# A sigmoid-attention, Fourier-mixing and feed-forward kernel: weight blocks start later, stores are put back, a shorter reciprocal root, one load for queries and keys, and another order of the first chunk's weight sums

## The chip, the cores and the metric

The kernel runs on one core of one Trainium2 chip. A core has five instruction streams that run on their own and meet at semaphores: TensorE (PE; its weight loads are listed as PEld), VectorE (DVE), ScalarE (ACT), GpSimd (POOL) and SyncE (SP), which here only issues transfers. Sixteen DMA engines carry the transfers. Each stream works in program order. The metric is the time of one execution on the device, in microseconds; lower is better.

## What is computed

There are 8 batches of 448 tokens, 12 heads of 64, a model width of 768 and a hidden width of 3072, all in float32.

```python
scores = scale * np.matmul(q, k.transpose(0, 1, 3, 2)) - np.log(S)
attn = 1.0 / (1.0 + np.exp(-scores))          # a sigmoid, no softmax
x = np.matmul(attn, v)                        # heads put side by side: [8, 448, 768]
mixed = np.real(np.fft.fft(np.fft.fft(x, axis=1), axis=2))
u = x + mixed
un = (u - mean(u)) / np.sqrt(var(u) + 1e-06)
out = u + np.maximum(un @ w_ch1, 0.0) @ w_ch2
```

## The kernel before

The program is one function. It has three stages on PE: attention with the Fourier mixing, a first chunk of 512 token rows in plain matrix products, and six further chunks in a scheme with seven products in place of eight.

**Attention runs in passes.** A pass is one group of two head pairs (gg), numbered from 0; there are 24, three to a batch. A pass is eight steps of a counter t, two to a turn of the loop at line 541. In the turns PE computes the scores (half_scores, scores), ACT their sigmoid, and PE the values of the pass before (half_values, values). Other work is put into a table of steps, at(t, fn), and each turn emits what stands there for its two steps. pin() then ties every instruction to the one before it on the same engine, SP included, so the order of emission is the order of execution on each stream.

Four kinds of work stand in that table.

*Queries and keys.* load_qk(g) brings one half group, keys and queries in two transfers, on SP (on ACT for g = 1). There are four buffers of each. cast (ACT, and DVE or POOL for the first two) rounds them, rest (DVE, line 119) keeps the remainder; the products of rounded and remainder parts make the scores.

*Weight blocks.* There are 48, 24 of each matrix. weight(n, step) handles one. Step 0 is SP's load of 768 KB into a buffer wr (four of them). Step 1, on ACT (line 300), takes the absolute values into a buffer wt (four, shared with the tiles hl of the normalization). Step 2, on DVE (line 305), takes the maximum over the block. Step 3, on DVE (lines 309, 312, 314), is three integer operations that put a float32 together, called the shifts here. Step 4 (line 317) is SP's store of 384 KB to t_dram. A block is named by its end, the step t of its shifts; ends lists t with the distances of the five steps from it. Before, there are three families: one end each eighth step from 11 on, one each eighth from 16 on, and one each 24th from 30 on. They are ordered by t, and the first 48 are used. After the last come weight_top (the maximum over all, DVE and a POOL all-reduce) at TP and weight_scales four steps later. pair loads two blocks back and splits them into a high and a low float16 part.

*Folds and mixing.* POOL folds the outputs of a batch (fold, lines 194 to 200). mix_units(b) lists the matrix products of the two Fourier transforms in small units; mix_some emits some 4.9 us of them at step 4 of a pass. Their constants are cd, cs and ident, loaded at steps 18 and 22; cs has 113 rows. The results are tiles u (three buffers), which SP stores to u_dram. sp_next holds these stores until flush(sp_next), which comes at the start of each turn.

*Normalization of chunk 0.* Two half chunks, at steps 96 and 120 and the 20 after each: norm loads u (n = 0), takes statistics (n = 1), the reciprocal root rsqrt (n = 2 to 6), scales (n = 7), splits into hl (n = 8 on ACT, line 401; n = 9 on DVE, line 405) and transposes by DMA on SP (line 407). rsqrt starts from an integer trick and makes four Newton rounds of four DVE operations each on 128 x 2 elements. fast_norm does the same for the later chunks, twice a chunk.

**The first chunk.** For each of 24 hidden blocks f, up_proj makes 18 products, evac the relu (ACT) and its low part (DVE), down_proj 24 products four blocks later. prepare(k) runs twice per block, at k = 2f and 2f + 1, called half steps, and takes the steps of pair due then from plan: load, high part (ACT, line 435), low part (DVE, line 437), four sums in place on POOL (line 445), high and low part of the sums, store to w_dram. The distances from 4p are listed in line 636; the second matrix (i = 1) follows 5 later. The rest of the last batch's mixing runs between the first four blocks (mix_rest). PSUM has two banks for up_proj and for the transposes of fast_norm (ps_h).

**The further chunks.** fast_up and fast_down run 28 products to a group; DVE and ACT combine their results, and fast_norm prepares the next chunk.

Of the kernel before, what the change touches and what calls it, by code (L numbers as in the profile page):

```python
# [9 lines left out]
F32 = mybir.dt.float32  # L10
# [3 lines left out]
ALU = mybir.AluOpType  # L14
# [4 lines left out]
S = 448  # L19
# [3 lines left out]
D = 64  # L23
# [28 lines left out]

def spectral_attention_ffn(tc, q, k, v, w1, w2, cd, cs, ident_in, out):
    nc = tc.nc
    B = q.shape[0]
    NT = B * S
# [5 lines left out]
    with ExitStack() as top:  # L62
# [19 lines left out]
        if True:  # L82
# [11 lines left out]

            def load_qk(g):
                b, n = divmod(g, 2 * NG)
                qr = io.tile([128, SQ], F32, tag="qr", name="qr", bufs=4)
                kr = io.tile([128, S], F32, tag="kr", name="kr", bufs=4)
                e = nc.scalar if g == 1 else nc.sync
                e.dma_start(kr, k[b, n])  # L100
                e.dma_start(qr, q[b, n])
                raw[g] = (qr, kr)

# [99 lines left out]
            def mix_units(b):  # L203
# [32 lines left out]
                def add_x(kp, r, hf):  # L236

                    lo, hi = (1, HM - 1) if r and not kp else (0, HM - kp)
                    s, d = sd[kp]
                    if hf == 0:  # L240
                        if kp and r:
                            flush(sp_next)
                        ut[kp, r] = fx.tile([128, DM], F32, tag="u", name="u", bufs=3)
                    u = ut[kp, r]
                    ps = ps_m.tile([128, 512], F32, tag="m", name="psx")
                    for i in range(3):
                        nc.tensor.transpose(
                            ps[:HM - kp, i * 128:(i + 1) * 128], xT[:, hf * 3 + i, r, kp:HS:2], ident)
                    y = d if hf == r else s
                    m = HM - kp  # L250
                    ysl = y[:m, 384:0:-1] if hf else y[:m, 0:384]

                    def add():
                        nc.vector.tensor_tensor(
                            out=u[:m, hf * 384:hf * 384 + 384], in0=ps[:m, :384], in1=ysl, op=ALU.add)
                        if hf:
                            base = b * S + (0, 113, 225, 336)[2 * r + kp] - lo

                            cut = lo + (hi - lo) // 16 * 16
                            for i, j in ((lo, cut), (cut, hi)):  # L260
                                if i < j:
                                    sp_next.append(lambda i=i, j=j: nc.sync.dma_start(
                                        u_dram[base + i:base + j, :], u[i:j, :]))
                    dve_next.append(add)
# [91 lines left out]
            def rsqrt(c, n):  # L356
                mv = mvs[c]
                a, r, t = (mv[:, n] for n in range(2, 5))
                if n == 2:
# [8 lines left out]
                    return  # L368
                k = UN_SCALE if n == 6 else 1.0
                nc.vector.tensor_tensor(out=t, in0=r, in1=r, op=ALU.mult)  # L370
                nc.vector.tensor_tensor(out=t, in0=t, in1=a, op=ALU.mult)
                nc.vector.tensor_scalar(  # L372
                    out=t, in0=t, scalar1=-0.5 * k, scalar2=1.5 * k, op0=ALU.mult, op1=ALU.add)
                nc.vector.tensor_tensor(out=r, in0=r, in1=t, op=ALU.mult)

# [6 lines left out]
            def norm(c, i, n, pool):  # L382
# [6 lines left out]
                elif n == 1:  # L389
                    stats(c, i % 2, uns[c, i])  # L390
                elif n < 7:
                    rsqrt(c, n)
# [16 lines left out]
            def norm_plan(c, g, pool):  # L409

                res = [(0, lambda: norm(c, 2 * g, 0, pool))]
                for j in range(2):
                    for n, t in ((1, 6 + j), (7, 10 + j), (8, 16 + 2 * j), (9, 18 + 2 * j)):
                        res += [(t, lambda i=2 * g + j, n=n: norm(c, i, n, pool))]
                res += [(8 + n // 4, lambda n=n: norm(c, 2 * g, n, pool)) for n in range(2, 7)]
                return sorted(res, key=lambda x: x[0])
# [71 lines left out]

            load_qk(0)
            load_qk(1)  # L490
            load_v(0)
            for g in range(2):
# [3 lines left out]
                rest(g, 1)  # L496
            load_qk(2)
            load_qk(3)
            load_v(1)
            TQ = 4 * G  # L500
            TP = TQ - 16
            extra = {}
# [10 lines left out]
            for gg in range(1, GG):  # L513
                if gg > 1:
                    at(8 * gg - 4, lambda n=gg: load_v(n))
                    at(8 * gg - 14, lambda g=2 * gg: load_qk(g))
                    at(8 * gg - 13, lambda g=2 * gg + 1: load_qk(g))
                for w in range(2):
                    for n, fn in enumerate((cast, rest)):
                        at(8 * gg - 4 + 2 * n + 2 * w, lambda g=2 * gg + w, fn=fn: (fn(g, 0), fn(g, 1)))  # L520
            at(18, lambda: nc.sync.dma_start(cd_sb, cd))
            at(22, lambda: (nc.sync.dma_start(cs_sb, cs), nc.sync.dma_start(ident, ident_in)))
            ends = sorted([(t, (-8, -3, -1, 0, 2)) for t in range(11, TP + 2, 8)]
                          + [(t, (-8, -5, -2, 0, 2)) for t in range(16, TP + 2, 8)]
                          + [(t, (-8, -4, -2, 0, 2)) for t in range(30, TP + 2, 24)])
            for n, (t, ds) in enumerate(ends[:2 * NFC]):
# [4 lines left out]
            at(TP + 4, weight_scales)  # L531
            for p, d in ((0, 0), (1, 3)):
                for step, e in enumerate((0, 8 + 4 * p, 9 + 4 * p)):
                    at(TP + d + e, lambda p=p, step=step: pair(0, p, step))
# [6 lines left out]
            for t in range(0, TQ + 12, 2):  # L541
                flush(sp_next)
                gg, part = divmod(t // 2, 4)
# [21 lines left out]
        with ExitStack() as fast, ExitStack() as st:  # L565
# [61 lines left out]
            def mix_rest(us):  # L627
                flush(sp_next)
                flush(act_next)
                flush(dve_next)  # L630
                mix_some(us)

            plan = {}
            for p in range(NP):
                for i in range(2):
                    for step, d in enumerate((-7, -4, -3, -2, -1, 0, 2)):
                        if i == 0 and p < 2 and step < 3:
                            continue
                        plan.setdefault(max(4 * p + d + 5 * i, min(step, 2)), []).append((step, i, p))

# [36 lines left out]
            def fast_norm(c, tp, n, ps_pool):  # L677
# [11 lines left out]
                if n < 3:  # L689
                    stats(c, n - 1, rows[n - 1])  # L690
                elif n < 8:
                    rsqrt(c, n - 1)
                elif n < 10:
                    scale_rows(c, n - 8, rows[n - 8])
# [259 lines left out]
def _layout(q, k, v, w1, w2):  # L954
# [5 lines left out]
    n = np.arange(HS)  # L960
    qt, kt = (np.ascontiguousarray(a) for a in (qt[..., np.concatenate([n, -n % S])], kt))
    vt = v.reshape(B, 2, NG, 2, S, D)
# [18 lines left out]
    for kp in range(2):  # L981
        ang = (n[:, None] * np.arange(kp, HS, 2)) % S
        half = np.where(n % 112 == 0, 0.5, 1.0)[:, None]
        for c, fn in enumerate((np.cos, np.sin)):
            m = fn(2 * np.pi * ang / S) * half
            m[(ang + 112 * (1 - c)) % 224 == 0] = 0.0
            cs[:, kp, c, :HM - kp] = m
    return {"q_in": qt, "k_in": kt, "v_in": vt, "w1_in": w1t, "w2_in": w2t, "cd_in": cd, "cs_in": cs,
            "id_in": np.eye(128, dtype=np.float32)}
# [28 lines left out]
```

## Time and profile before

| | us |
|---|---|
| median of 3 runs | 1635.09 |
| lowest and highest | 1633.77, 1635.5 |
| the profiled execution | 1633.69 |
| its span, first to last instruction | 1631.9 |
| PE busy | 1579.4 (97%) |
| DVE busy | 1290.7 (79%) |
| ACT busy | 676.3 (41%) |
| POOL busy | 286.9 (18%) |

The times count one execution; the profile is another single execution, so sums made from its rows are compared with its own time. All times in rows are microseconds from the start of the span unless ns is written. The table of busy time by stretch gives for each stretch its length, then the busy time and, in brackets, the number of instructions of PE, PEld, DVE, ACT and POOL, then the granted PE clock as a share of full speed, the DMA engines' mean busy share and the GB/s moved. A line of the timeline gives start, duration, engine, line of the kernel, operation, output and input, count, and in square brackets how long the engine had been idle and what ended that. A group's line gives busy time, mean ns of one, and the idle time before it. The DMA lines give KB and the median time from issue to landing. SPq is the instruction with which SP issues a transfer.

### The profile page before, as it was taken

What the parts mean: (1) busy time and instruction counts of PE and PEld (TensorE: products, weight loads), DVE (VectorE), ACT (ScalarE), POOL (GpSimd) and SP (SyncE); (2) the same over time, 40 slices, a digit from 0 to 9 for tenths busy, and PEclk for the clock granted to TensorE, in tenths of its full rate; (3) what the DMA queues carried; (4) which work ended last, traced back from release to release, by engine and by line L of the source; (5) the groups of instructions that cost most, each with busy time, mean ns of one, the idle gap of its engine ahead of it and who ended that gap; (6) DMA issues with size and microseconds to landing.
All of it is one profiled execution on the core that took longest, in us unless ns stands there. A gap on an engine that the chain in (4) does not pass through costs nothing.

```text
span 1631.9 us, 28066 instructions
## 1 busy us (share of the span) xinstructions
PE 1579.4 (97%) x11176; PEld 1084.1 (66%) x11176; DVE 1290.7 (79%) x2527; ACT 676.3 (41%) x903; POOL 286.9 (18%) x245
## 2 busy tenths in 40 slices
PE   8699988899998999999999999999999999999998
PEld 3355655465654557777777777777777777777775
DVE  6687798874687865788878888888889888887778
ACT  7577766576345441423233323332333233323221
POOL 3334433344677640000000000000000000000000
PEclk9799999999999999999999999999999999999999
DMA  8788978872587886555566657564756475656561
GB/s 283 245 294 290 313 227 285 284 264 87 196 329 285 301 313 269 213 208 228 219 244 221 242 185 280 206 257 154 304 199 231 180 280 208 238 204 242 204 255 60
DMA packets 85557, 388.68 MB, mean 238 GB/s; under 512 B 14913, under 2 KB 28466, under 8 KB 66866
## 3 DMA queue, kind: packets, MB, share of 16 engines
q1 hardware_dynamic: 85138, 386.43, 64.8%
q8 instruction: 87, 1.43, 0.3%
q10 hardware_dynamic: 288, 0.46, 0.1%
q14 instruction: 44, 0.36, 0.1%
HBM read 311.36 MB, written 73.92 MB: 236 GB/s over the span
## 4 chain that ended last, share of the span: by engine, by line
PE 66%; DVE 4%; POOL 1%; issue 1%; ACT 1%; DMA 0%; ACTq 0%; DVEq 0%; POOLq 0%
PE pso L826 29%; PE psf L770 29%; PE po L600 4%; PE psh L580 3%; DVE wp L437 1%; POOL wq L445 1%; PE pst L699 1%; DVE F L776 1%; DVE H L776 0%; ACT H L805 0%; DVE ur L621 0%; DVE ur L854 0%; DVE mv L370 0%; DVE acc L903 0%; DVE mv L372 0%
## 5 line engine op out<-in xcount | busy, mean ns | idle before, releaser
L826 PE MATMUL pso<-ws,H 128*128 128x384 f16 x3024 | 507.5, 326 | 1.0 <-DVE H L776 0.9
L770 PE MATMUL psf<-ut,ws 128*128 128x256 f16 x4536 | 506.6, 273 | 1.2 <-DVE ur L621 1.2
L770 PEld LDWEIGHTS <-ws 128*128 128x128 f16 x4536 | 443.8, 98 | 60.3 <-issue 1.7
L826 PEld LDWEIGHTS <-H 128*128 128x128 f16 x3024 | 295.6, 98 | 186.9 <-DVE H L776 1.7
L795 ACT ACTIVATE F<-F 128x1024 f32<-128x1024 f32 x72 | 76.1, 1056 | 400.7 <-DVE F L776 400.7
L841 DVE TENSOR_TENSOR acc<-pso,acc 128x384 f32<-128x384 f32 x399 | 206.9, 548 | 21.7 <-PE pso L826 21.7
L776 DVE TENSOR_TENSOR H<-F,H 128x1024 f16<-128x1024 f32 (+1 forms) x144 | 155.2, 1086 | 54.3 <-ACT H L805 54.3
L124 ACT ACTIVATE a<-sc 128x900 f32<-128x900 f32 x168 | 147.3, 920 | 56.7 <-PE sc L136 50.1
L805 ACT ACTIVATE H<-F 128x1792 f16<-128x1792 f32 x72 | 122.2, 1697 | 106.7 <-DVE F L776 106.7
L776 DVE TENSOR_TENSOR F<-X,psf 128x256 f32<-128x256 f32 x288 | 117.3, 417 | 56.2 <-PE psf L770 52.7
L445 POOL TENSOR_TENSOR wq<-wq 128x384 f32<-128x384 f32 x96 | 129.6, 1353 | 63.6 <-DVE wp L437 38.6
L776 DVE TENSOR_TENSOR F<-F 128x256 f32<-128x256 f32 x288 | 109.3, 421 | 20.4 <-ACT F L795 15.3
L174 PE MATMUL av<-a,vr 128*64 128x450 f32 x576 | 120.0, 553 | 0.0
L580 PE MATMUL psh<-ut,wp 128*128 128x512 f16 x432 | 101.0, 386 | 5.3 <-ACT U L700 4.2
L776 DVE TENSOR_TENSOR X<-X,psf 128x256 f32<-128x256 f32 x216 | 89.5, 414 | 16.9 <-PE psf L770 12.8
L437 DVE SCALAR_TENSOR_TENSOR wp<-wq,wsc,wp 128x1536 f16<-128x1536 f32 x48 | 92.0, 1943 | 11.2 <-ACT wp L435 11.1
L435 ACT ACTIVATE wp<-wq,wsc 128x1536 f16<-128x1536 f32 x48 | 74.2, 1571 | 63.3 <-POOL wq L445 58.8
L194 POOL TENSOR_TENSOR eo<-xT 128x450 f32<-128x450 f32 x47 | 51.0, 1106 | 239.6 <-ACT xT L182 230.0
L600 PE MATMUL po<-wp,hh 128*128 128x256 f16 (+1 forms) x384 | 88.6, 326 | 0.0
L784 ACT ACTIVATE X<-psf 128x256 f32<-128x256 f32 x72 | 27.8, 386 | 141.9 <-PE psf L770 141.9
L174 PEld LDWEIGHTS av<-a,vr 128*64 128x64 f32 x576 | 37.4, 137 | 71.2 <-issue 71.2
L580 PEld LDWEIGHTS <-wp 128*128 128x128 f16 x432 | 42.9, 99 | 56.7 <-issue 9.8
(88 smaller groups left out, 1686.5 us busy)
## 6 DMA issues: line engine op xcount, KB each, us to landing
ws<-w_dram SPq DMA_DIRECT2D x144, 1344.0 KB, 7.2
wr<-w_in SPq DMA_DIRECT2D x48, 768.0 KB, 7.4
w_dram<-wp SPq DMA_DIRECT2D x24, 1344.0 KB, 10.2
t_dram<-wt SPq DMA_DIRECT2D x48, 384.0 KB, 3.2
wq<-t_dram SPq DMA_DIRECT2D x24, 768.0 KB, 5.1
vr<-v_in SPq DMA_DIRECT2D x24, 448.0 KB, 7.8
qr<-q_in SPq DMA_DIRECT2D x47, 225.0 KB, 4.1
kr<-k_in SPq DMA_DIRECT2D x47, 224.0 KB, 4.3
```

Source lines behind the costliest of these rows:

```text
L124: nc.scalar.activation(a, ps[:, :, :SQ], AF.Sigmoid, bias=-math.log(S), scale=1.0 / math.sqrt(D))
L174: nc.tensor.matmul(ps[j * D:(j + 1) * D, :SQ], vr[:, h:h + D], a[:, j], start=False, stop=(c == 2))
L437: nc.vector.scalar_tensor_tensor(out=w[:, 1, part], in0=t, scalar=sc, in1=w[:, 0, part], op0=ALU.mult, op1=ALU.subtract)
L445: nc.gpsimd.tensor_tensor(out=t[:, o], in0=t[:, x], in1=t[:, y], op=op)
L580: nc.tensor.matmul(hs[c, f], l[:, m], r[:, m], start=(m == n == 0), stop=(m == NCC - 1 and n == 2))
L600: nc.tensor.matmul(po[n][:, at:at + hi - lo], l[:, cols], r[:, lo:hi], start=(f == 0 and m == 0 and at == 0), stop=(f == NFC - 1 and m == ...
L770: nc.tensor.matmul(ps[:, :TH], w[:, x, a, m * 128:(m + 1) * 128], ut[y][:, b, m], start=(m == n == 0), stop=(m == n == 2))
L776: nc.vector.tensor_tensor(out=o, in0=x, in1=y, op=op)
L795: nc.scalar.activation(F[:, 0:4], F[:, 0:4], AF.Relu)
L805: nc.scalar.activation(hts[P][:, 0], F[:, 1:8], AF.Copy)
L826: nc.tensor.matmul(ps[:, :384], H[:, x, a, tp * 128:(tp + 1) * 128], w[:, y, b], start=(j == n == 0 and half != 1), stop=(j == 1 and n == ...
L841: later(0, lambda: nc.vector.tensor_tensor(out=to, in0=ps[:, :384], in1=to, op=ALU.add))
```

## The change

Seven things are done.

1. The weight blocks' ends move. Before, by step 32 eight loads had been issued (steps 3, 8, 11, 16, 19, 22, 24, 27); after, four (11, 19, 24, 27). The first family now starts at end 19, the second at 32, and the third is one end in each pass from 46 to 70 and from 150 to 174. weight_top moves from step 176 to 180, and the loads and conversions of the first two pairs with it.
2. The store of a block comes four steps after its shifts, not two. The stores of u are emitted at the first turn of a pass only, and there are four u buffers; in the rest of the mixing four stores stay in the list as long as units remain.
3. rsqrt makes three Newton rounds of three operations, by means of an operation with two tensor inputs and a scalar.
4. Queries and keys of both halves of a group lie side by side in memory, and one load of 128 rows of 7184 bytes fetches them into one of two buffers. The first group's is cut in two halves, one on SP and one on ACT.
5. In the first chunk's plan the high part, the low part and the sums of a pair come one half step earlier, and the second matrix follows 6 half steps after the first; so its last three steps (high and low part of the sums, store) come one later.
6. The last round's factor in rsqrt, 1.0, is left out, and the step numbers that called it.
7. The inputs are laid out to match (host side).

```diff
-            def load_qk(g):
-                b, n = divmod(g, 2 * NG)
-                qr = io.tile([128, SQ], F32, tag="qr", name="qr", bufs=4)
-                kr = io.tile([128, S], F32, tag="kr", name="kr", bufs=4)
-                e = nc.scalar if g == 1 else nc.sync
-                e.dma_start(kr, k[b, n])
-                e.dma_start(qr, q[b, n])
-                raw[g] = (qr, kr)
+            def load_qk(gg, parts=1):
+                b, r = divmod(gg, NG)
+                t = io.tile([128, 2 * (SQ + S)], F32, tag="qk", name="qk")
+                for w in range(2):
+                    o = w * (SQ + S)
+                    raw[2 * gg + w] = (t[:, o:o + SQ], t[:, o + SQ:o + SQ + S])
+                step = 2 * (SQ + S) // parts
+                for x in range(parts):
+                    cols = slice(x * step, (x + 1) * step)
+                    (nc.scalar if x else nc.sync).dma_start(t[:, cols], qk[b, r][:, cols])
...
-                        if kp and r:
-                            flush(sp_next)
-                        ut[kp, r] = fx.tile([128, DM], F32, tag="u", name="u", bufs=3)
+                        ut[kp, r] = fx.tile([128, DM], F32, tag="u", name="u", bufs=4)
...
-                k = UN_SCALE if n == 6 else 1.0
                 nc.vector.tensor_tensor(out=t, in0=r, in1=r, op=ALU.mult)
-                nc.vector.tensor_tensor(out=t, in0=t, in1=a, op=ALU.mult)
-                nc.vector.tensor_scalar(
-                    out=t, in0=t, scalar1=-0.5 * k, scalar2=1.5 * k, op0=ALU.mult, op1=ALU.add)
-                nc.vector.tensor_tensor(out=r, in0=r, in1=t, op=ALU.mult)
+                nc.vector.scalar_tensor_tensor(
+                    out=t, in0=t, scalar=-0.5, in1=a, op0=ALU.mult, op1=ALU.mult)
+                nc.vector.scalar_tensor_tensor(
+                    out=r, in0=t, scalar=1.5, in1=r, op0=ALU.add, op1=ALU.mult)
...
-            TP = TQ - 16
+            TP = TQ - 12
...
-                    at(8 * gg - 14, lambda g=2 * gg: load_qk(g))
-                    at(8 * gg - 13, lambda g=2 * gg + 1: load_qk(g))
+                    at(8 * gg - 14, lambda g=gg: load_qk(g))
...
-            ends = sorted([(t, (-8, -3, -1, 0, 2)) for t in range(11, TP + 2, 8)]
-                          + [(t, (-8, -5, -2, 0, 2)) for t in range(16, TP + 2, 8)]
-                          + [(t, (-8, -4, -2, 0, 2)) for t in range(30, TP + 2, 24)])
+            ends = sorted([(t, (-8, -3, -1, 0, 4)) for t in range(19, TP, 8)]
+                          + [(t, (-8, -5, -2, 0, 4)) for t in range(32, TP, 8)]
+                          + [(t, (-8, -4, -2, 0, 4)) for t in (46, 54, 62, 70, 150, 158, 166, 174)])
...
-            for p, d in ((0, 0), (1, 3)):
-                for step, e in enumerate((0, 8 + 4 * p, 9 + 4 * p)):
+            for p, d in ((0, 0), (1, 1)):
+                for step, e in enumerate((0, 8 + p, 9 + p)):
...
             for t in range(0, TQ + 12, 2):
-                flush(sp_next)
+                if t % 8 == 0:
+                    flush(sp_next)
...
             def mix_rest(us):
-                flush(sp_next)
+                while len(sp_next) > (4 if units else 0):
+                    sp_next.pop(0)()
...
-                    for step, d in enumerate((-7, -4, -3, -2, -1, 0, 2)):
+                    for step, d in enumerate((-7, -5, -4, -3, -1, 0, 2)):
...
-                        plan.setdefault(max(4 * p + d + 5 * i, min(step, 2)), []).append((step, i, p))
+                        plan.setdefault(max(4 * p + d + 6 * i, min(step, 2)), []).append((step, i, p))
```

More of the change, by code (lines that the diff above doesn't have):

```diff
@@ L50, with spectral_attention_ffn @@
 HI_MIN = 1.125 * 2.0 ** -15
-def spectral_attention_ffn(tc, q, k, v, w1, w2, cd, cs, ident_in, out):
+def spectral_attention_ffn(tc, qk, v, w1, w2, cd, cs, ident_in, out):
     nc = tc.nc
-    B = q.shape[0]
+    B = qk.shape[0]
     NT = B * S
@@ L390, in norm @@
                     stats(c, i % 2, uns[c, i])
-                elif n < 7:
+                elif n < 6:
                     rsqrt(c, n)
@@ L414, in norm_plan @@
                         res += [(t, lambda i=2 * g + j, n=n: norm(c, i, n, pool))]
-                res += [(8 + n // 4, lambda n=n: norm(c, 2 * g, n, pool)) for n in range(2, 7)]
+                res += [(8 + n // 4, lambda n=n: norm(c, 2 * g, n, pool)) for n in range(2, 6)]
                 return sorted(res, key=lambda x: x[0])
@@ L487, in pin @@
                 seen[0] = len(ins)
-            load_qk(0)
-            load_qk(1)
+            load_qk(0, 2)
             load_v(0)
@@ L496, in spectral_attention_ffn @@
                 rest(g, 1)
-            load_qk(2)
-            load_qk(3)
+            load_qk(1)
             load_v(1)
             TQ = 4 * G
-            TP = TQ - 16
+            TP = TQ - 12
             extra = {}
@@ L690, in fast_norm @@
                     stats(c, n - 1, rows[n - 1])
-                elif n < 8:
+                elif n < 7:
                     rsqrt(c, n - 1)
+                elif n == 7:
+                    pass
                 elif n < 10:
@@ L960, in _layout @@
     n = np.arange(HS)
-    qt, kt = (np.ascontiguousarray(a) for a in (qt[..., np.concatenate([n, -n % S])], kt))
+    qk = np.concatenate([qt[..., np.concatenate([n, -n % S])], kt], axis=-1)
+    qk = np.ascontiguousarray(qk.reshape(B, NG, 2, 2 * D, SQ + S).transpose(0, 1, 3, 2, 4)).reshape(B, NG, 2 * D, -1)
     vt = v.reshape(B, 2, NG, 2, S, D)
@@ L987, in _layout @@
             cs[:, kp, c, :HM - kp] = m
-    return {"q_in": qt, "k_in": kt, "v_in": vt, "w1_in": w1t, "w2_in": w2t, "cd_in": cd, "cs_in": cs,
+    return {"qk_in": qk, "v_in": vt, "w1_in": w1t, "w2_in": w2t, "cd_in": cd, "cs_in": cs,
             "id_in": np.eye(128, dtype=np.float32)}
@@ L1003 @@
     arrays = _layout(*(np.asarray(inputs[n]) for n in ("q", "k", "v", "moe_w_ch1", "moe_w_ch2")))
-    B = arrays["q_in"].shape[0]
+    B = arrays["qk_in"].shape[0]
     nc = bacc.Bacc("TRN2", target_bir_lowering=False, num_devices=1, dynamic_dma_scratch_size=1024)
```

## The prediction

> **What bounds the kernel now.** I read busy time by stage first, cut where the first up-projection and the first fast product start on PE. Columns: stretch, length, then busy time of PE, PE's weight loads, DVE, ACT and POOL, granted clock, DMA share, GB/s.
>
> ```profile
> 0.00:412.98 412.98, 373.19 (x2385) 216.57 (x2385) 306.80 (x490) 277.18 (x405) 158.98 (x151) 0.96 0.76 255
> 412.98:625.46 212.48, 205.83 (x1114) 114.19 (x1113) 157.96 (x169) 94.76 (x96) 127.92 (x95) 0.99 0.76 278
> 625.46:1631.90 1006.44, 1000.40 (x7680) 753.30 (x7680) 825.91 (x1869) 304.32 (x402) 0.00 (x0) 1.00 0.59 223
> ```
>
> PE sets the time: 6.0 us idle in the last 1006, 6.7 in the middle, 39.8 in attention. The change leaves PE's work alone, so it can win those gaps and the slow clock after them. Next, attention by pass (one pass is one group, eight steps t).
>
> ```profile
> 37.78:64.50 26.72, 13.18 (x80) 6.25 (x80) 14.57 (x18) 12.48 (x19) 9.64 (x9) 0.72 0.75 265
> 97.25:112.31 15.06, 14.61 (x103) 8.18 (x99) 13.05 (x24) 11.69 (x18) 5.94 (x6) 1.00 0.98 342
> 112.31:128.24 15.93, 15.93 (x111) 10.18 (x106) 13.22 (x20) 11.31 (x18) 5.62 (x5) 1.00 0.88 283
> 222.89:245.15 22.26, 18.26 (x109) 10.36 (x104) 20.18 (x38) 13.22 (x21) 5.91 (x6) 0.92 0.66 203
> 245.15:264.94 19.79, 16.53 (x103) 9.03 (x99) 16.29 (x28) 12.29 (x19) 7.04 (x7) 0.91 1.05 368
> 280.86:301.08 20.22, 16.97 (x109) 9.62 (x104) 18.49 (x29) 12.99 (x21) 5.88 (x6) 1.00 0.67 198
> 301.08:322.55 21.47, 17.42 (x103) 9.31 (x99) 17.00 (x29) 12.73 (x20) 7.12 (x7) 0.84 0.96 323
> ...
> 25.98 1.08 PE L149 MATMUL sc<-qr,kr 64*64 64x450 f32 x8
> 37.78 1.08 PE L149 MATMUL sc<-qr,kr 64*64 64x450 f32 x8
> ```
>
> A pass with mixing costs 15.93 or (each third) 15.06 us with PE full; one without costs 37.78 - 25.98 = 11.8. So pass 3 loses 26.7 - 11.8 = 14.9, and passes 14, 15, 17 and 18 lose 6.3, 4.7, 4.3 and 6.4, 21.7 together. The page's chain only says PE 66%; the timeline names the causes.
>
> **Pass 3: a transfer on one engine.**
>
> ```profile
> 30.73 0.42 SPq L521 DMA_DIRECT2D cd_sb<-cd_in  x1
> ...
> 37.43 0.35 SPq L522 DMA_DIRECT2D cs_sb<-cs_in  x1
> 56.29 0.89 ACT L300 ACTIVATE wt<-wr 128x768 f32<-128x768 f32 x1 [8.98 <-DMA wr<-w_in]
> 58.21 0.89 ACT L300 ACTIVATE wt<-wr 128x768 f32<-128x768 f32 x1 [1.03 <-DVE wt L305]
> 60.40 0.74 PE L136 MATMUL sc<-qh,kh 64*128 64x450 f32 x2 [12.14 <-ACT a L124]
> 61.00:62.00 1.00, 1.00 (x8) 0.91 (x6) 0.34 (x1) 1.00 (x4) 0.92 (x2) 0.50 0.06 25
> ...
> cs_sb<-cs_in SPq DMA_DIRECT2D x1, 199.5 KB
> wr<-w_in SPq DMA_DIRECT2D x48, 768.0 KB, 7.4
> ```
>
> ACT waits for a weight block, its sigmoids stand behind that, and PE behind them. More is in it than volume: at 61 us the DMA share is 0.06, one engine of sixteen, at 25 GB/s. I take that to be the one that carried cs (113 rows): 204 KB at 25 GB/s is 8.2 us, and every later load has a piece behind it. The change thins the weights ahead of cs but leaves cs.
>
> New ledger. When cs is issued, the queue holds what was sent from about 30 us on: a query-key pair (920 KB), cd (1.19 MB), one block (0.79 MB), the values (0.46 MB). At 288 to 400 GB/s (mean of these passes; 16 engines at 25) cs starts at 38.4 to 41.4 and ends at 46.6 to 49.6. Behind it, a store and the block of step 24 take 3 us of that engine (24 and 48 KB): block at 49.6 to 52.6, against 56.29. PE followed 4.1 us later, with two block steps on ACT in between; now one, 2.2 us. PE resumes at 51.8 to 54.8: **gain 5.6 to 8.6, I take 7**. Ends: 3 (cs starts no sooner) and 15.9 (ACT never waits; a microsecond of slow clock with it).
>
> **Passes 14 to 18: VectorE.**
>
> ```profile
> 206.16 0.70 DVE L119 TENSOR_TENSOR ql<-qr,qh 128x450 fp32r<-128x450 f32 x1
> 216.37 1.94 POOL L194 TENSOR_TENSOR eo<-xT 128x450 f32<-128x450 f32 x2 [9.99 <-ACT xT L182]
> 216.44 0.95 DVE L360 TENSOR_SCALAR mv<-mv 128x2 f32<-128x2 f32 x1
> ...
> 224.52 0.16 DVE L374 TENSOR_TENSOR mv<-mv 128x2 f32<-128x2 f32 x1
> 229.81 0.47 PE L136 MATMUL sc<-ql,kh 64*128 64x450 f32 x2 [3.17 <-DVE ql L119]
> 235.05 0.33 SPq L317 DMA_DIRECT2D t_dram<-wt  x1
> 235.47 2.71 SPq L407 DMA_TRANSPOSE ut<-hl  x2
> 235.80 0.95 DVE L405 TENSOR_TENSOR hl<-un,hl 128x768 f16<-128x768 f32 x1
> 237.66 0.93 ACT L300 ACTIVATE wt<-wr 128x768 f32<-128x768 f32 x1 [3.69 <-DMA t_dram<-wt]
> ...
> L309 DVE TENSOR_SCALAR wt<-wt 128x768 int32<-128x768 int32 x48 | 28.3, 590 | 0.6
> L312 DVE SCALAR_TENSOR_TENSOR wt<-wr,wt 128x768 int32<-128x768 int32 x48 | 46.8, 974 | 1.7
> L314 DVE SCALAR_TENSOR_TENSOR wt<-wr,wt 128x768 int32<-128x768 int32 x48 | 47.6, 992 | 1.7
> ```
>
> DVE works without a gap from 206.16 to 235.80 and falls 9 us behind: PE waits for ql, the block's store comes late, and ACT waits for its buffer. The third family of blocks now skips steps 72 to 146, so one block's shifts go from the stretch: 0.59 + 0.97 + 0.99 = 2.55. The root had 3 + 4 x 4 = 19 operations in 8.2 us, for it met POOL's folds (0.95 beside them, 0.16 and a gap of 0.04 alone). It now has 3 + 3 x 3 = 12 and starts 2.5 earlier, at 213.9: 2.4 us, done before 216.37. What slides into the folds instead (maxima, scalings, shifts and ql: four at the 0.8 that the root's rows differ by) pays about 3.0: net 2.8. DVE reaches L405 5.3 us sooner, at 230.5.
>
> Now against it. With its store two steps later, block 112's store (step 116) stands on SP behind the transposes of step 114, which wait for L405; the block of step 115 needs its buffer, as all four are then held (two blocks, two hl). So: L405 ends 231.4, a transpose 1.3 (half of 2.71), the next block load and the values 1.1, the store's issue 0.3, landing 2.6 (235.05 to 237.66): ACT goes on at 236.7 instead of 237.66. Pass 14 wins only about 1.4 of 6.3. Pass 15's blocks were late behind the transposes; with one block fewer I give it 4.2 of 4.7. Pass 17 repeats this with 2 us less lost, so less backlog: I give 3 of 4.3. Pass 18 is as pass 15: 5.5 of 6.4. Sum **14.1, I take 14**, ends 4 (pass 14's share in all: 1.4 of 6.3) and 21.7.
>
> [...]
>
> **The crowded steps.** Blocks that leave the first steps come back at ends 46 to 70 and 150 to 174: three a pass.
>
> ```profile
> 210.32 0.38 SPq L292 DMA_DIRECT2D wr<-w_in  x1
> 214.94 0.92 ACT L300 ACTIVATE wt<-wr 128x768 f32<-128x768 f32 x1 [1.95 <-DVE wt L309]
> ...
> 175.13:222.89 47.76, 46.62 (x313) 28.19 (x309) 38.78 (x66) 34.98 (x53) 18.92 (x20) 1.00 0.83 289
> DMA to landing us min/median/max: 4.5/7.4/11.0
> ```
>
> With four buffers, the load at step 48 needs the block loaded at 38, whose shifts stand at 46; likewise at 56, 64, 152, 160, 168. Pass 13 has one such load, late behind the third family's store: it leaves at 210.32, ACT waits 1.95 after a landing of 4.6, and passes 11 to 13 lose 47.76 - 2 x 15.93 - 15.06 = 0.8 at most. With the median 7.4 the wait is 4 to 5; the 3.69 at 237.66 left 22.26 - 18.26 - 3.17 = 0.8 us of idle PE beside the 3.17. DVE is busy 13.2 of 15.9 in pass 7 at seven blocks to three passes; two thirds of a block more, at 2.55 for shifts and 0.95 for a maximum, make 15.5, so it can't catch up. Pass 6 will move about 5.6 MB (three blocks and stores, 1.35 MB of q, k, v, half the mix stores): 372 GB/s over 15.06, where 342 kept the queue 0.98 busy. I charge 1.5 each for three early loads, nothing for late ones: **5 lost**, ends 0 and 40 (rival d).
>
> **First chunk.**
>
> ```profile
> 492.35 13.09 POOL L445 TENSOR_TENSOR wq<-wq 128x384 f32<-128x384 f32 x8 [2.68 <-ACT hh L587]
> 499.90 3.04 ACT L435 ACTIVATE wp<-wq,wsc 128x1536 f16<-128x1536 f32 x2 [6.68 <-POOL wq L445]
> 503.47 5.66 PE L580 MATMUL psh<-ut,wp 128*128 128x512 f16 x18 [4.18 <-ACT U L700]
> 513.30 4.05 PE L580 MATMUL psh<-ut,wp 128*128 128x512 f16 x18
> ```
>
> ACT waits for POOL's sums, the bank comes free late, PE waits 4.18 and runs slow (5.66 for 4.05), 5.8 in all. The sums now stand one half step, 4 us (half of 513.30 - 503.47 less the slow 1.6), further ahead of their conversion. 6.68 becomes 2.6, which two banks cover: **gain 5**, ends 2 and 7 (the stage's 6.7). Both conversions of an odd half step (2 x 1.5) now precede that block's relu; the bank is wanted a block, 8 us, later: 0, at worst 3.
>
> **Edits at nothing.** Twelve of 14 roots lie in the last stage, under a PE 99% busy. Four q/k loads in one move the same bytes; the one load needs both halves of its buffer free, the last two steps ahead of it as before, and is read ten steps later; at the start both halves land together, so kh can't start first: 0, from -0.4 to 0.4 at the 5.28 where PE starts. u stores wait for every fourth loop pass: readers come 40 steps later, and the fourth u buffer covers them. weight_top, the scales and the pairs move up to four steps; on POOL the all-reduce now stands behind the last group's first folds (two at about 1 us, 216.37's row), and its readers follow four steps later; pair 0's conversion ends near step 189, and PE's first use of it, at 412.98, is after 202. Four stores kept back on SP in the rest of the mix cost 0.
>
> Sum: 7 + 14 + 5 - 5 = 21 off the profiled execution's 1633.7 (span 1631.9 and 1.8 around it): 1612.7. The median shown is 1.4 above it, so **1614**.
>
> **Rivals.**
> (a) All cover holds: pass 3 wins 15, norm 20, chunk 7, nothing is crowded: 1633.7 - 42 + 1.4, 1593. For: DVE has room once the third family is out. Against: cs's 0.06 row. 0.15.
> (b) The late store keeps the norm passes: 4 instead of 14, 1624. For: SP's order and the 3.69 wait. 0.22.
> (c) cs sets pass 3 whatever precedes it (3), and crowding takes 9: 13 won, 1622. 0.10.
> (d) Slower: the crowded steps. If blocks land 11 us after issue (the maximum), ACT waits 7 to 8 at six loads; PE loses 5 to 7 each, DVE's backlog adds: 40 lost against 26 won, 1649; it turns slower above 26 lost, 4.3 a load. For: 0.98 of the queue in pass 6 already. Against: the median is 7.4, and waits of 2 to 4 us cost PE under one. 0.06.
> (e) The gains are undone nearly exactly: 1635. 0.03.
>
> Forecast 0.44, with a range of its own of 1605 to 1623. Eight in ten need (b), (c) and most of (a): 1597 to 1628. Measurement tells apart about 0.2%, 3.3 us. Faster 0.91, same 0.03, slower 0.06.
>
> **What will show it.** Pass 3 near 20 us, cs still ending alone at a 0.06 share. The root with 0.16 us rows. ACT waiting about 7 us for t_dram in pass 14, 2 to 3 in 17. Waits for wr in passes 6 to 8. No 6 us wait of ACT on POOL after 420. Wrong if pass 3 is 12 us (cs doesn't matter), or if passes 6 to 8 or 19 to 21 exceed 19 us.

## The result, and the profile after

| | before | after |
|---|---|---|
| median, us | 1634.43 (4 runs, 1633.7 to 1635.5) | 1648.06 (4 runs, 1647.23 to 1650.28) |
| the profiled execution's span, us | 1631.9 | 1648.5 |
| granted PE clock, mean of the span | 0.988 | 0.982 |

The changed kernel is slower, by 0.85%: ratio 1.0085, interval 1.0067 to 1.0102. I had predicted 1614, in a range of 1597 to 1628.

First the table of busy time by stretch of the kernel after: pass 3; passes 6 to 9; 14 to 18; 19 to 21; and from pass 23's start to the first fast product (the columns are those of the prediction's first fence).

```profile
38.39:59.62 21.23, 12.73 (x80) 6.25 (x80) 9.71 (x11) 11.62 (x18) 7.93 (x8) 0.76 0.72 261
91.39:169.91 78.52, 68.56 (x410) 39.57 (x406) 62.81 (x96) 47.56 (x71) 26.33 (x24) 0.91 0.74 262
232.63:321.79 89.16, 82.10 (x515) 48.86 (x510) 72.57 (x125) 60.50 (x91) 29.99 (x30) 0.94 0.91 279
321.79:384.24 62.45, 52.59 (x312) 30.63 (x308) 47.62 (x72) 36.85 (x56) 18.76 (x18) 0.89 0.75 263
400.15:642.06 241.91, 231.91 (x1267) 129.48 (x1260) 170.27 (x178) 107.73 (x116) 162.72 (x111) 0.98 0.70 248
```

The same table of the kernel before, for passes 6 to 9, 14 to 18 and 19 to 21:

```profile
97.25:159.20 61.95, 61.04 (x410) 36.28 (x406) 49.80 (x83) 46.62 (x70) 24.81 (x24) 1.00 0.90 305
222.89:322.55 99.66, 85.11 (x515) 48.49 (x511) 87.08 (x154) 62.31 (x94) 31.88 (x30) 0.93 0.82 270
322.55:369.35 46.80, 46.35 (x313) 28.07 (x308) 34.63 (x57) 33.98 (x51) 19.20 (x18) 1.00 0.76 253
```

Same work of PE, other lengths. Pass 3 won 26.72 - 21.23 = 5.5, passes 14 to 18 won 10.5. Passes 6 to 9 lost 16.6 and 19 to 21 lost 15.7, 32.2 together, where I had charged 5. The stretch from pass 23 to the fast products, 240.2 before (625.46 less 385.23), lost 1.7; passes 4, 5 and 10 to 13 won 2, the first three lost 0.6, and the last thousand microseconds did not move. That is -5.5 - 10.5 + 32.2 + 1.7 - 2 + 0.6 = 16.5, of the 16.6 by which the span grew. Each length is that of one profiled execution.

**What the crowded passes wait for** stands in the table of waits of the kernel after (engine and line, what it waited for, us in total, times, longest; the table covers the whole kernel):

```profile
ACT wt L300 <- DMA t_dram<-wt: 30.7, 5, 7.7
PE pss L226 <- ACT xT L184: 20.0, 6, 4.5
ACT wt L300 <- DMA ut<-hl: 12.7, 2, 6.9
PE psx L247 <- DVE u L254: 10.8, 3, 6.0
ACT wt L300 <- DMA wr<-w_in: 9.0, 1, 9.0
```

I had looked for waits of ACT for the load of wr. They are absent here but for pass 3's one. ACT waits for a *store*, t_dram<-wt: it wants a free buffer wt. All five of these waits lie in the crowded passes, 12.5 us in passes 6 to 9 and 18.2 in 19 to 21; the two for ut are those of passes 14 and 17. The timeline of passes 7 and 8 shows how (SPq is SP issuing a transfer):

```profile
115.72 0.35 SPq L104 DMA_DIRECT2D qk<-qk_in  x1
116.13 0.42 SPq L317 DMA_DIRECT2D t_dram<-wt  x1
118.14 0.33 SPq L292 DMA_DIRECT2D wr<-w_in  x1
124.56 0.90 ACT L300 ACTIVATE wt<-wr 128x768 f32<-128x768 f32 x1 [5.77 <-DMA t_dram<-wt]
...
143.76 0.89 ACT L300 ACTIVATE wt<-wr 128x768 f32<-128x768 f32 x1 [6.76 <-DMA t_dram<-wt]
145.14 1.63 PE L226 MATMUL pss<-A,cs_sb 113*113 113x385 f32 x2 [3.54 <-ACT xT L184]
```

At step 59 the blocks with ends 54, 56, 59 and 62 hold all four buffers. ACT wants one for the block of end 64, and the first to come free is that of 54. Its store, four steps after its shifts, stands at step 58, where SP first issues a query-key load of 898 KB. The store is issued at 116.13 and ACT is released 8.4 us later. Behind ACT's wait stands the copy of an attention output (xT, line 184), and for that the mixing's products on PE wait (3.54 at 145.14). The page's list of transfers has the delay as a median:

```profile
t_dram<-wt SPq DMA_DIRECT2D x48, 384.0 KB, 7.3
```

Before, that median was 3.2.

### The profile page after: what moved, and what is told of

Read it like the earlier page. It is cut to its first block, busy times and chain, and to the rows that moved or that the text cites. A ratio compares the mean times of both kernels' runs of the same rounds, so it can differ in the third digit from the quotient of the medians.

```text
span 1648.5 us, 27777 instructions
## 1 busy us (share of the span) xinstructions
PE 1590.1 (96%) x11176; PEld 1090.9 (66%) x11176; DVE 1276.9 (77%) x2429; ACT 674.9 (41%) x903; POOL 300.8 (18%) x245
## 4 chain that ended last, share of the span: by engine, by line
PE 65%; DVE 3%; DMA 2%; ACT 1%; issue 0%; ACTq 0%; DVEq 0%; SPq 0%
PE pso L826 29%; PE psf L770 29%; PE po L597 4%; PE psh L577 3%; DMA wq<-t_dram 2%; PE pst L699 1%; DVE wp L436 1%; DVE F L776 1%; ACT wp L434 1%; DVE H L776 0%; ACT H L805 0%; DVE ur L618 0%; DVE ur L854 0%; DVE acc L903 0%; DVE acc L841 0%
## 5 line engine op out<-in xcount | busy, mean ns | idle before, releaser
L444 POOL TENSOR_TENSOR wq<-wq 128x384 f32<-128x384 f32 x96 | 144.3, 1507 | 48.6 <-issue 21.9
L436 DVE SCALAR_TENSOR_TENSOR wp<-wq,wsc,wp 128x1536 f16<-128x1536 f32 x48 | 95.3, 2019 | 11.6 <-ACT wp L434 11.5
L196 POOL TENSOR_TENSOR eo<-xT 128x450 f32<-128x450 f32 x47 | 48.2, 1047 | 253.5 <-ACT xT L184 246.5
L121 DVE TENSOR_TENSOR ql<-qk,qh 128x450 fp32r<-128x450 f32 x48 | 37.2, 775 | 57.7 <-ACT qh L114 44.7
```

Of the source, the lines that this page charges most:

```text
L436: nc.vector.scalar_tensor_tensor(out=w[:, 1, part], in0=t, scalar=sc, in1=w[:, 0, part], op0=ALU.mult, op1=ALU.subtract)
L444: nc.gpsimd.tensor_tensor(out=t[:, o], in0=t[:, x], in1=t[:, y], op=op)
```

## The experiments

Theory 1: the late store, with four buffers and three blocks a pass, makes the loss. Theory 2, the rival: three blocks a pass are too much for the loads of wr or for DVE, whenever they are stored, as my prediction priced it. All runs below start from the kernel after unless they are said to start from the kernel before. Ratios are to the kernel before, run beside them (medians 1631.8 to 1632.6). The intervals reach 0.1 to 0.2% to each side, so two runs that are less than some 4 us apart are hardly told apart by their times; there the lengths of the passes have to say more.

**e1, the store back at two steps.**

```diff
-            ends = sorted([(t, (-8, -3, -1, 0, 4)) ...
+            ends = sorted([(t, (-8, -3, -1, 0, 2)) ...   # likewise in the other two families
```

> The changed kernel with one part undone: a weight block's store stands two steps after its shifts again, not four. Theory 1 (in the passes with three blocks all four wt buffers are held, and the late store stands on SP behind the query-key load, so ACT waits 5 to 8 us for it): passes 6 to 9 and 19 to 21, which lose 32 us against full passes, lose 10 at most; 1648 becomes 1620 to 1630. Theory 2 (three blocks a pass are too many for DVE or the queue, wherever the store stands): the passes keep 25 us or more of the loss; 1642 to 1650.

Measured 1624.81, ratio 0.9956 (0.9936 to 0.9975): 23 us less than the kernel after. The table of stretches of e1, for passes 6 to 9, 14 to 18 and 19 to 21:

```profile
92.14:159.46 67.32, 62.89 (x411) 36.06 (x406) 60.94 (x94) 47.44 (x71) 26.95 (x24) 1.00 0.84 299
222.24:306.63 84.39, 78.18 (x514) 45.17 (x510) 74.50 (x124) 60.24 (x91) 31.18 (x30) 1.00 0.89 295
306.63:360.24 53.61, 50.04 (x312) 29.03 (x308) 49.40 (x73) 37.39 (x57) 21.89 (x19) 0.94 0.86 305
```

The crowded passes give back 11.2 + 8.8 = 20.0 of 32.2. Passes 14 to 18 win another 4.8; there the same buffers are shared with the normalization. But 12.2 us of crowding stay with the store in time, 2 more than theory 1 allowed. The table of waits of e1, over the whole kernel:

```profile
ACT wt L300 <- DMA wr<-w_in: 24.6, 9, 10.1
ACT wt L300 <- DMA t_dram<-wt: 9.8, 2, 5.1
```

The second line is passes 14 to 18 alone: in the crowded passes no wait for the store is left. Of the first, 10.1 is pass 3's. Inside the crowded passes the same table has, for passes 6 to 9 and then for 19 to 21:

```profile
ACT wt L300 <- DMA wr<-w_in: 3.7, 2, 2.1
ACT wt L300 <- DVE wt L305: 3.6, 1, 3.6
ACT wt L300 <- DVE wt L309: 2.3, 1, 2.3
...
ACT wt L300 <- DMA wr<-w_in: 9.3, 3, 3.4
```

So what is left is waits for loads of wr and waits that the profile puts down to DVE. How the 12.2 divide between the two is not shown.

**e2, the store late, but the third family spread out.**

```diff
-   for t in (46, 54, 62, 70, 150, 158, 166, 174)])
+   for t in (30, 46, 62, 78, 94, 142, 158, 174)])
```

> The changed kernel with its stores, but the third family's eight ends 30, 46, 62, 78, 94, 142, 158, 174, so that no two passes in a row have three blocks and a block never needs the buffer of the third family's last one. Theory 1: the waits of ACT for t_dram go, 25 of the 32 us come back, 1620 to 1630. Theory 2: each of the eight passes still loses what a pass with three blocks costs, 3 us or more, 1635 to 1645.

Measured 1626.96, ratio 0.9971 (0.9959 to 0.9982). Its table of stretches, same passes:

```profile
94.86:157.65 62.79, 61.24 (x410) 35.88 (x406) 56.94 (x86) 46.88 (x70) 28.05 (x24) 1.00 0.86 310
221.40:317.68 96.28, 82.63 (x514) 48.73 (x510) 78.75 (x129) 61.26 (x91) 33.16 (x31) 0.91 0.83 268
317.68:364.56 46.88, 46.43 (x313) 27.79 (x309) 39.44 (x59) 35.79 (x54) 19.45 (x18) 1.00 0.82 294
```

With the same late store and three blocks only in every second pass, passes 6 to 9 and 19 to 21 cost 62.8 + 46.9, within 1 us of before. So in these passes the late store costs about nothing by itself, and crowding by itself costs 12 (e1); the two together cost 32. Beside the normalization it is another matter. What e2 wins here it pays in passes 14 to 18, 7.1 us more than the kernel after. The end 142, which the kernel after does not have, puts a third block into pass 17, and ACT waits 5.1 there for a store; that pass takes 26.6 in place of 22.7.

**e4, a fifth buffer wt, all else as after.**

```diff
-    t = wpre.tile([128, DM], F32, tag="wt", name="wt", bufs=4)
+    t = wpre.tile([128, DM], F32, tag="wt", name="wt", bufs=5)   # and hl, X, which share them
```

> The changed kernel with five wt buffers in place of four (shared by blocks and hl, and by X in the last stage), stores and ends as changed. Theory 1: ACT's waits for t_dram in passes 6 to 8 and 19 to 21 and for the transposes in 14 and 17 go or fall under 2 us; 25 of 32 us and 5 to 9 in passes 14 and 17 come back: 1612 to 1622. Theory 2: 1640 to 1650.

Measured 1624.63, ratio 0.9954 (0.9934 to 0.9973), 2.6 above the upper end expected. No wait of ACT for t_dram or for ut is left in its table of waits, though the store's median landing is 7.5 us: the buffer was short, not the queue too slow. Passes 6 to 9 and 19 to 21:

```profile
91.24:159.71 68.47, 63.65 (x411) 37.29 (x406) 66.17 (x96) 47.93 (x71) 31.40 (x24) 0.95 0.86 302
306.44:357.37 50.93, 48.26 (x314) 28.55 (x309) 49.98 (x72) 37.20 (x56) 23.29 (x18) 0.97 0.87 310
```

They take 68.5 and 50.9, so 10.6 of crowding stay here too. ACT waits only 2.9 for wr in them, and PE waits 7.5 for DVE's u, in three waits.

**e3 and b_cs, cs in two loads**, in the kernel after and in the kernel before.

```diff
-   nc.sync.dma_start(cs_sb, cs)
+   nc.sync.dma_start(cs_sb[:HM - 1], cs[:HM - 1])
+   nc.sync.dma_start(cs_sb[HM - 1:], cs[HM - 1:])
```

> The changed kernel with cs loaded as 112 rows and one row in place of 113 rows in one transfer. Theory cs (the 113 rows run on one DMA engine, and every later load waits for its piece behind them): pass 3 falls from 21.2 us to 12 to 14, the stretch at a DMA share of 0.06 goes, the time falls 7 to 9 to about 1640. Rival (pass 3 is short of bytes in all): pass 3 stays at 19 to 22 and the time within 2 us of 1648.

> The kernel before with one edit: cs loaded as 112 rows and 1 row. Theory 1 (the 113 rows go through one DMA engine and hold every later load): pass 3 falls from 26.7 to 12 to 15 us although eight blocks are still asked for by step 32; time 1617 to 1623. Rival (the volume of the early blocks sets pass 3, as part of my prediction had it): pass 3 stays at 19 to 24 us, time 1626 to 1632.

e3: 1637.87, ratio 1.0039 (1.0018 to 1.006), from 8 runs that spread from 1631.68 to 1644.04; 10.2 less than the kernel after, where 7 to 9 were expected. b_cs: 1625.38, ratio 0.9956 (0.994 to 0.9972); its profiled execution, 1621.22, is the fastest of its four. The tables of stretches, pass 3 of e3:

```profile
38.02:50.90 12.88, 11.23 (x80) 5.04 (x76) 8.23 (x9) 10.34 (x16) 6.53 (x7) 1.00 1.01 367
```

and pass 3 of b_cs:

```profile
38.25:56.57 18.32, 13.15 (x80) 6.27 (x80) 14.49 (x18) 12.48 (x19) 9.65 (x9) 0.83 0.99 382
```

Pass 3 takes 26.7 (before), 21.2 (fewer blocks), 18.3 (cs in two loads), 12.9 (both): 5.5 and 8.4 apart, 13.8 together. They add up. For b_cs neither side was right: without the long transfer the volume still costs 6.5 over the 11.8 of a pass without mixing. The 8.4 is about the 8.2 us that I had given one engine for 204 KB at 25 GB/s.

**e5, store at two steps and cs in two loads.**

> The kernel after with two edits: the store two steps after the shifts, and cs loaded as 112 rows and 1 row. Theory 1 (a late store behind the query-key load and one transfer on one DMA engine are separate losses): the gains add up. The store alone gave 1624.8 with pass 3 at 22.5 us; pass 3 falls to 12 to 14, so 1612 to 1617. Rival (pass 3's gain is given back in the crowded passes, since the same blocks then come sooner): passes 6 to 9 exceed 72 us together, 1620 to 1625.

Measured 1612.31, ratio 0.988 (0.9865 to 0.9894); pass 3 is 13.1 us long. The gains add up, as theory 1 had it. Passes 6 to 9 take 70.7, so the rival saw a little of it: 3.4 more than in e1.

**e6, the all-reduce earlier.** In the kernel after, PE stands 5.95 us at the end of attention. Its timeline, POOL's and PE's rows:

```profile
392.11 0.98 POOL L196 TENSOR_TENSOR eo<-xT 128x450 f32<-128x450 f32 x1 [10.27 <-ACT xT L184]
403.80 0.37 POOL L323 PARTITION_ALL_REDUCE ws<-wm  x1 [10.70 <-issue]
411.17 0.98 POOL L196 TENSOR_TENSOR eo<-xT 128x450 f32<-128x450 f32 x1 [7.00 <-issue]
...
429.33 2.29 PE L247 MATMUL psx<-ident,xT 128*112 128x128 f32 x9 [5.95 <-DVE u L254]
```

The all-reduce is 0.37 us of work with 10.70 before and 7.00 behind it in which POOL does nothing: some 18 us, between the first and the second fold of the last batch. The folds behind it come late. DVE's share of them waits for POOL (2.87 us at 423.13, 2.91 at 426.68), the additions of u stand behind those, and PE's transposes want their banks. The run e6 puts the maximum and the all-reduce at step 176, where they were before, on the store at two steps; the maximum leaves out the last block.

```diff
-            at(TP, weight_top)
+            at(TP - 4, weight_top)
```

> The kernel after with the store at two steps, and the maximum over all blocks with its all-reduce at step 176 instead of 180; the maximum leaves out the last block. Theory 3 (the all-reduce holds POOL some 18 us; at step 180 it falls among the last batch's folds, so the last u tiles and PE come late): PE's wait for DVE's u at the end of attention (5.3 us with the store at two steps) falls under 3, time 1620 to 1623 against 1624.8. Rival (VectorE's own work is late there): the wait stays at 5 to 6, time 1624 to 1626.

Measured 1621.14, ratio 0.9932 (0.9917 to 0.9947): 3.7 less than e1, and the longest wait for u went from 5.3 to 2.5. The stretch from pass 23 to the first fast product is 237.0 long. It is 237.0 to 237.5 in the three runs with the early all-reduce and this plan (e6, e12, e14), and 238.8 to 242.9 in the seven with the late one, this plan and the shorter root (the kernel after, e1 to e5, e11). POOL's rows in e6:

```profile
365.38 0.37 POOL L323 PARTITION_ALL_REDUCE ws<-wm  x1 [6.46 <-DVE wm L321]
375.03 2.44 POOL L196 TENSOR_TENSOR eo<-xT 128x450 f32<-128x450 f32 x2 [9.27 <-ACT qh L114]
```

Here the idle time lies where POOL has nothing to do anyway.

**e8, the old root.** The four rounds of before, on the store at two steps (the diff is the change's own, reversed).

> The kernel after with the store at two steps and the four-round root of before. Theory 4 (the shorter root is worth about half of what the normalization passes won): passes 14 and 17 together are 4 to 6 us longer than 38.3, passes 15 and 18 up to 2 longer than 30.1; time 1628 to 1632. Rival (the weight blocks taken out of those passes did it): passes 14 to 18 within 1.5 us, time 1624 to 1626.

Measured 1627.59, ratio 0.9968 (0.9955 to 0.9981), 2.8 above e1. Passes 14 and 17 take 40.5 together against 38.3, passes 15 and 18 the same as in e1: the root is worth 2.2 of the 15.3 us that e1 won in passes 14 to 18. The other runs with the store at two steps and four buffers have 38.2 to 38.6 in passes 14 and 17, so this is clear of their spread; the 2.8 by itself is not. That lies between the two expectations and nearer the rival. The rest of the gain I put down to the blocks that left, by subtraction: no run has them back with the new root.

**e9 and e13, the old plan of the first chunk**, with the all-reduce late (against e1) and early (against e6).

```diff
-   for step, d in enumerate((-7, -5, -4, -3, -1, 0, 2)):   ...  4 * p + d + 6 * i
+   for step, d in enumerate((-7, -4, -3, -2, -1, 0, 2)):   ...  4 * p + d + 5 * i
```

> The kernel after with the store at two steps and the first chunk's plan of before (sums one half step later, second matrix 5 half steps after the first). Theory 5 (the new order is worth the 5 us I predicted): PE's wait of about 4 us for the bank in the first chunk comes back, the stretch from pass 23 to the first fast product grows from 240.0 to 243 to 246; time 1627 to 1631. Rival (what the order wins it gives back elsewhere in that stretch): 239 to 241.5, time 1623.5 to 1626.

> The kernel after with the store at two steps, the all-reduce at step 176 (last block left out of the maximum) and the first chunk's plan of before. Against e6 (1621.1, stretch from pass 23 to the first fast product 236.9) only the plan differs. Theory 7 (the new plan is a gain once the all-reduce is out of its way): PE's gaps in the later blocks grow from 1.2 to 3 to 6 us, the wait of 2.5 in the mixing goes; stretch 238 to 240, time 1622 to 1625. Rival (the new plan is a loss by itself, as the run with the old plan and the late all-reduce said, 237.1 against 240.0): stretch 233 to 235.5, time 1617.5 to 1620.

e9: 1621.47, ratio 0.9932 (0.9916 to 0.9947), 3.3 less than e1; against the expectation. But its all-reduce also came 2 us sooner after pass 23's start, and PE's wait for u fell to 2.9. e13, where only the plan differs from e6: 1620.57, ratio 0.9925 (0.991 to 0.994), against 1621.14. That is no difference, and neither side was right. The tables of stretches from pass 23 on, e6 (new plan) first:

```profile
389.00:437.00 48.00, 43.03 (x214) 26.15 (x207) 28.63 (x36) 21.14 (x24) 24.97 (x21) 0.93 0.49 171
437.00:610.60 173.60, 172.42 (x953) 93.48 (x951) 137.02 (x130) 76.45 (x78) 124.57 (x80) 1.00 0.83 297
```

then e13 (old plan):

```profile
391.60:439.60 48.00, 45.17 (x236) 27.41 (x229) 27.62 (x35) 19.48 (x24) 26.28 (x22) 0.96 0.55 172
439.60:613.10 173.50, 170.20 (x933) 91.86 (x931) 137.32 (x131) 79.08 (x79) 113.11 (x78) 0.99 0.81 297
```

The new plan leaves PE 173.60 - 172.42 = 1.2 idle in the later blocks where the old one leaves 3.3. In the 48 us of mixing ahead of them it leaves 5.0 where the old one leaves 2.8, and PE does 214 products there in place of 236. Two microseconds are won and two lost; the stretch is 237.0 long in both.

**e10, the old stores of u**: at each turn, three buffers, all sent at once in the rest of the mix, on the store at two steps.

> The kernel after with the store at two steps and the u stores of before: emitted at each turn, three u buffers, all of them sent at once in the rest of the mix. My prediction costed this edit at nothing: 1623.5 to 1626, crowded passes as with the store alone. Rival (the u stores in one bunch at the head of a pass delay the query-key and weight loads behind them): passes 9, 20 and 21 (17.7, 17.2 and 20.5) fall by 3 or more together, time 1619 to 1622.

Measured 1627.52, ratio 0.9971 (0.9959 to 0.9982): 2.7 above e1, outside both expectations, but the two intervals overlap. The profiled execution is the slowest of its seven (1631.37) and 6.8 above e1's: 4.0 of it lies in passes 6 to 9 (71.3 against 67.3) and 2.8 from pass 23 on (242.8 against 240.0, with 242.9 in e4, which has the new stores). So a gain of the new way of storing u, which I had costed at nothing, is possible and not shown; the loss that the rival looked for is not there.

**e11, e12, e14 and e15: toward a better kernel.** e11 adds five buffers wt to e5. e12 adds an earlier first family, a spread third one, and the all-reduce at step 176 with all blocks in it. e14 starts the first family at 19 again, with the third at other ends. e15 is e14 with the old plan.

> The kernel after with the store at two steps, cs loaded as 112 rows and 1 row, and five buffers wt. Theory 1 (buffers of wt and nothing else hold passes 14 and 17): these fall from 38.2 together to 32 to 34; passes 8, 9, 20 and 21 (18.7, 20.4, 17.2, 18.1), which wait for VectorE with the store in time, stay above 70 together; time 1608 to 1612 against 1612.3. Rival (those four passes also wait for wt): they fall to 64 to 66, time 1600 to 1606.

> As the run before (store at two steps, cs in two loads, five buffers wt), with the first family from end 11, the third at 30, 38, 46, 62, 78, 94, 150 and 166, and the maximum with its all-reduce at step 176. Theory 6 (three blocks in each of several passes in a row are more than VectorE does beside the mixing; in every second pass they fit): passes 6 to 9 and 19 to 22 at 15.0 to 16.5 each, PE's wait for u at the end of attention under 3; time 1596 to 1603. Rival (the two blocks brought back to the first steps fill the queue again): pass 3 at 16 to 20 us, time 1603 to 1609.

> The kernel after with the store at two steps, cs in two loads, five buffers wt, the maximum at step 176, the first family from end 19, the third at 30, 46, 54, 62, 78, 94, 102, 150 and 166. Theory 6 (the block loads brought back to the first steps cost passes 3 to 6 in the run before, not the spread of the third family): pass 3 12.5 to 14, passes 4 to 6 at 15 to 16, 7 to 9 at most 17; time 1600 to 1606. Rival (DVE is short in pass 6 and 7 with three blocks again): passes 6 to 9 above 68 together, 1607 to 1612.

> As the run before with the first chunk's plan of before. Theory 7: 1.5 to 3 us slower than the run before. Rival: 1.5 to 3 us faster.

| | us | ratio (interval) | pass 3 | passes 6 to 9 | 14 to 18 | 19 to 21 |
|---|---|---|---|---|---|---|
| e5 | 1612.31 | 0.988 (0.9865 to 0.9894) | 13.1 | 70.7 | 84.2 | 51.2 |
| e11 | 1613.20 | 0.9886 (0.9865 to 0.9906) | 12.7 | 68.0 | 84.6 | 49.5 |
| e12 | 1610.74 | 0.9872 (0.9857 to 0.9887) | 15.9 | 64.7 | 85.0 | 48.5 |
| e14 | 1611.77 | 0.9875 (0.986 to 0.9889) | 15.3 | 65.2 | 86.7 | 48.2 |
| e15 | 1611.33 | 0.9868 (0.9851 to 0.9884) | 16.3 | 65.0 | 86.9 | 50.1 |

All beat the kernel before by some 20 us and the kernel after by some 35, and none beats another; the old plan of e15 makes no difference to e14 in time, as in e13. e14's time lies in the rival's range, though not for its reason (passes 6 to 9 at 65.2); the other three missed theirs. The parts that were expected came in the main: in e11 passes 14 and 17 fell from 38.2 to 33.6, in e12 and e14 the two crowded stretches came down by 8.8 and 8.5 together. Each time other passes gave most of it back. In e11, 15 and 18 rose from 30.1 to 35.1 together: what passes 14 and 17 won was lost in the next ones. In e12 and e14 pass 3 grew by 2.8 and 2.3. The 48 blocks have to go somewhere, and each place that was tried has its price.

## Why the prediction was wrong

**The crowded steps: the step that failed.** It had the place right, "With four buffers, the load at step 48 needs the block loaded at 38", but it counted wr's buffers and not wt's. It charged "1.5 each for three early loads, nothing for late ones". Measured: 32.2 us. Of this 20 belong to buffers of wt held by a store that comes late (e1, and e4 with no wait for it left), and 12 to the crowding that I had charged 5 (e1, where waits for wr, which I had looked for, are a part). From a forecast 21 us down to a span 16.6 us up it is 37.6 us, and 27.2 of them are this step. The sign that I had named for it came: passes 6, 8, 20 and 21 took 20.6, 21.3, 23.0 and 22.0 us, beyond the 19. I had worked out the late store's price in passes 14 and 17, where it stands behind transposes, and had not carried it to the passes where the same buffer meets three blocks. There the store is two steps, some 4 us, later, and lands 7.3 us after its issue, not 3.2; ACT's longest wait is 7.7. Rival (d) had 1649, within 1 us, by luck: it had 40 lost against 26 won, where 32 were lost and some 16 won, and its cause, loads landing at their maximum, was not the one.

**Pass 3: right.** 7 predicted; 5.5 came in pass 3 and about 1 in pass 4. The block was looked for at 49.6 to 52.6 and PE at 51.8 to 54.8. The timeline of the kernel after has them 1 us beyond those ranges:

```profile
53.40 0.89 ACT L300 ACTIVATE wt<-wr 128x768 f32<-128x768 f32 x1 [8.96 <-DMA wr<-w_in]
55.59 0.74 PE L138 MATMUL sc<-qh,kh 64*128 64x450 f32 x2 [8.50 <-ACT a L126]
```

The stretch with one engine at work is there too, from 55 to 61 us, as its table of stretches shows at 58 us:

```profile
58.00:59.00 1.00, 1.00 (x10) 0.36 (x12) 1.00 (x2) 0.80 (x2) 1.00 (x1) 0.50 0.06 25
```

**Passes 14 to 18: right in kind, 10.5 of 14.** By pass: 1.8 won in 14 (1.4 predicted), 4.8 in 15 (4.2), 6.5 in 18 (5.5), but 2.5 *lost* in 17 (3 gained predicted). There ACT waits 6.95 for the transposes out of hl, where I had allowed 2 to 3. The timeline of the kernel after, passes 14 and 17:

```profile
245.14 0.89 ACT L300 ACTIVATE wt<-wr 128x768 f32<-128x768 f32 x1 [5.77 <-DMA ut<-hl]
...
297.77 0.89 ACT L300 ACTIVATE wt<-wr 128x768 f32<-128x768 f32 x1 [6.95 <-DMA ut<-hl]
299.15 1.63 PE L226 MATMUL pss<-A,cs_sb 113*113 113x385 f32 x2 [3.61 <-ACT xT L184]
```

The buffer awaited is the one shared by blocks and normalization, as I had it, only held by hl rather than by the store; with five buffers (e4) passes 14 and 17 fall to 16.8 and 15.9. The root did not come out of the folds whole, for they began 1.5 us after it (225.15 and 223.62). The timeline of the kernel after, DVE:

```profile
224.41 0.16 DVE L370 SCALAR_TENSOR_TENSOR mv<-mv 128x2 f32<-128x2 f32 x1
...
225.20 0.95 DVE L372 SCALAR_TENSOR_TENSOR mv<-mv 128x2 f32<-128x2 f32 x1
226.18 0.91 DVE L369 TENSOR_TENSOR mv<-mv 128x2 f32<-128x2 f32 x1
```

Three of its twelve operations still met them (the third, 0.83, at 227.32); it took 4.5 us against my 2.4 and the 8.2 of before. Its own worth is 2.2 (e8). What is missing of the 14 was lost in pass 17. Two small figures of my sum do not come out of its own working: ACT at 236.7 in place of 237.66 is 1.0 us, not 1.4, and 1.4 / 6.3 of 21.7 is 4.8, not 4.

**The first chunk: the gap went, the gain did not come.** The 4.18 us wait of PE is 0.3 now, as predicted, and in its place stand two waits for u, 5.95 and 2.48. The plan by itself is worth nothing (e13 against e6, e15 against e14): what it wins in the later blocks it loses in the mixing ahead, which I had not looked at.

**Edits at nothing.** One was not. The all-reduce, put on POOL among the last folds, costs 3 to 4 us (e6); I had counted the folds ahead of it and not POOL's idle time around it. For the stores of u no worth is shown (e10). The rest was not tried by itself, the merged query-key load among it. That the store stands behind that load is seen in the timeline; how much of the 7.3 us is due to it is not shown, for e1 moves the store both ahead of it and earlier (4.1 there, but 6.1 in e10 with the same store step).

## What to carry to other kernels

When a release (a store, a transpose, a last reader) is put later, list every holder of that buffer at each step, from the instruction that fills it to the *landing* of the transfer that frees it; then see whether the steps that get more work are those where the list is full. A late release and a crowded step together can cost more than their sum (about 0 and 12 in these passes, 32 together). And after a gain, look at the pass behind it: in e11 to e15 what one pass won was mostly lost in others. DVE was busy 61 of 67 us in passes 6 to 9 of e1, so it had little room there; that it is the reason was not tried.

## What the runs showed of the hardware

With cs loaded as 113 rows, a stretch of pass 3 runs at a DMA share of 0.06, one engine of sixteen, and 25 GB/s (the row of 58 us, and that of 61 us before the change). With cs as 112 rows and 1 row pass 3 took 8.4 us less, 26.7 to 18.3 (b_cs) and 21.2 to 12.9 (e3), and in e3's pass 3 no stretch of several us at a share of 0.06 is left: its mean share is 1.01, where the kernel after has 0.72. That it is the load of 113 rows that ran on the one engine is my reading of these numbers; no row says which engine carries a transfer, and why it would be a single one is not shown.

In the kernel after an all-reduce of 0.37 us held POOL for some 18 (10.70 before it, 7.00 behind). A configuration of POOL is recorded at 393.1 and its operand was ready at 394.0, yet it started at 403.80, and the next ordinary operation came 7.00 after it. So there is a gap on both sides of the operation, 9.8 from the operand to the start and 7.0 behind; what POOL does in them is not shown.

The root's small operations on DVE, 0.16 or 0.17 us alone, took 0.83 to 0.98 beside POOL's folds in the first half chunk, those with one tensor input before (0.95 in the row of 216.44) as well as those with two now (0.95 in the row of 225.20).
